# Splitting each of the last two output stores into one of 119 rows and one of 9

## The chip, the cores and the metric

The kernel runs on one core of one Trainium2 chip. The metric is device time in microseconds (us) of one execution, as the median of several runs. One further execution was recorded by the hardware profiler; its page and its trace are what the readings below come from.

## What is computed

Two blocks follow each other. The first is a gated linear attention over 4 batches, 8 heads, 768 steps and head size 48. The second projects its output to 2 x 512 channels, runs a decaying sum over time on one half, gates it with the other half and projects back to 384 columns.

```
# attention: q, k, v, alpha are (B=4, H=8, S=768, D=48)
for t in range(S):
    state = alpha[:, :, t, :, None] * state + einsum('bhd,bhe->bhde', k[:, :, t], v[:, :, t])
    y[:, :, t] = einsum('bhd,bhde->bhe', q[:, :, t], state)
x = y.transpose(0, 2, 1, 3).reshape(B, S, H * D)          # (4, 768, 384)

# gated state-space block: w_in (384, 1024), A_log (512,), w_out (512, 384), float64 weights
val, gate = split(x @ w_in)                                # two halves of 512
h = exp(A_log) * h + val[:, t, :]                          # for every t; ys[:, t] = h
out = (gate * sigmoid(gate) * ys) @ w_out                  # (4, 768, 384) float32
```

Only the last lines matter for this change: the output is 4 x 768 rows of 384 float32 values, 1536 bytes a row, contiguous in DRAM.

## The kernel before

The work is cut into N = 12 groups of GC = 256 time steps (three groups for each batch), and each group into two chunks of C = 128 rows. The function `fast` writes out by hand one order of instructions for all engines; nothing reorders them afterwards. Each engine takes its own instructions in that order and waits on semaphores where data come from another engine or from a DMA. The attention of group m = n + 1 is interleaved with the state-space block of group n, so that TensorE always has matmuls to do. For the last group, n = 11, there is no attention left, and only the state-space block runs.

For each group, `output(n)` is called last. It takes two accumulators `os[0]` and `os[1]`, one for each chunk of 128 rows, and multiplies the gated hidden state `fs[n]` by `w_out`: the first three of four blocks of 128 channels in `part(range(split))`, the fourth in `finish()`. `finish` then copies each accumulator into an SBUF tile `o_sb` of 128 partitions x 384 values and stores it by a DMA that the SyncE queue (SP) issues:

- For all groups but the last, ScalarE does the copy (line 839) and SP stores it (line 842).
- For the last group, VectorE does the copies (line 841), and SP stores them with the same line 842.

The stores are line 842 throughout: 24 of them, two for each group, each of 128 rows. Each row is one packet of 1536 bytes for a DMA engine, and each engine that takes part in a transfer ends its share with a packet of 4 bytes, which counts up the semaphore of that transfer. Transfers that SP issues use a handful of semaphores in turn; in the program those of the last two stores are number 104 and number 107.

After the last group, `fast` returns a flag that was computed on the way: whether the inputs lie in the range for which this fast path is exact. The caller branches on it:

```
    with tc.manual_schedule():
        good = fast(tc, *args)
    with tc.If(good <= 0):
        general(tc, *args)
```

The flag is good here, so every engine jumps over the whole of `general` with one branch instruction (line 1059). At the target of that branch SP waits, one semaphore after the other, until every DMA has landed (line 1059), then for the other engines (line 1086), and then all engines meet at a last barrier. This is how the program ends; nothing is computed after the two copies of line 841.

Of the kernel before, what the change touches and what calls it, by code (L numbers as in the profile page):

```python
# [346 lines left out]
def fast(  # L347
# [18 lines left out]
    nc = tc.nc  # L366
# [3 lines left out]
    C = 128  # L370
    G = 2
    GC = G * C
    NG = S // GC
    N = B * NG
# [20 lines left out]
    def mm(*dims, b=None):  # L395
        return ps.tile([C, *dims], FP32, tag=f"b{b or next(next_mm)}", name="mm")
# [427 lines left out]
    def output(n):  # L824
        b, g = divmod(n, NG)
        os = [mm(DM) for c in range(G)]

        def part(ccs):
            for c in range(G):
                for cc in ccs:  # L830
                    nc.tensor.matmul(os[c], fs[n][:, cc, ds(c * C, C)], w_out[:, cc, :],  # L831
                                     start=(cc == 0), stop=(cc == NI - 1))

        def finish():
            part(range(split, NI))
            for c in range(G):
                o_sb = p3.tile([C, DM], FP32, tag="o_sb", name="o_sb")
                if n < N - 1:
                    nc.scalar.activation(o_sb, os[c], AF.Copy)  # L839
                else:  # L840
                    nc.vector.tensor_copy(out=o_sb, in_=os[c])
                nc.sync.dma_start(out=out[b, ds(g * GC + c * C, C), :], in_=o_sb)

        split = NI - 1 if n else NI // 2
        part(range(split))
        return finish
# [244 lines left out]
```

## Time and profile before

| what | value |
|---|---|
| median of 3 runs | 295.99 us (295.86 to 297.54) |
| the profiled execution, its own time | 295.81 us |
| its span, first to last instruction | 294.1 us |
| TensorE busy | 280.9 us, 96% of the span |
| mean granted TensorE clock | 0.998 |
| stores of line 842 | 24 of 192 KB each |

The span is what the views of the profile are counted in: time 0 is its first instruction. The difference between the profiled execution's own time and its span, 295.81 - 294.1 = 1.7 us, lies around the span. In the views, PE is TensorE, PEld its weight loads, DVE VectorE, ACT ScalarE, POOL GpSimd and SP SyncE; a q after the name means the engine's instruction queue, for instance a DMA that SPq issues. DMA transfers are shown by queue: the q1 transfers are those that SP issues, and the queues called instruction bring the engines their own program. A row "DMA" in digits gives the mean busy share of the core's 16 DMA engines in tenths, in 40 equal slices of the window that is shown.

### The profile page before, as it was taken

To read this page: it belongs to the slowest core of one execution; us is meant where nothing else is said; L and a number is where in the kernel's file an instruction comes from. 1 tells how busy PE (TensorE), PEld (TensorE's weight loads), DVE (VectorE), ACT (ScalarE), POOL (GpSimd) and SP (SyncE) were. 2 spreads that over 40 slices of the span, in tenths; PEclk is the share of its full clock that TensorE was granted. 3 is DMA by queue.
4 is the path that set the end of the run, shared out by engine and by line. 5 is a ranking of instruction groups with operands and counts; after the bars stand their busy time and mean duration, and the time that the engine had idled before them with its cause. 6 is when DMAs were issued, how large, how long until landed. Compare 5 with 4: busy or idle time off the path is not lost.

```text
span 294.1 us, 6126 instructions
## 1 busy us (share of the span) xinstructions
PE 280.9 (96%) x2345; PEld 226.1 (77%) x2345; DVE 224.9 (76%) x269; ACT 99.5 (34%) x220; POOL 113.7 (39%) x116
## 2 busy tenths in 40 slices
PE   7679999999999999999999999999999999999991
PEld 6468877886886896886886896886886886886870
DVE  5898896999996799798699699699699695312311
ACT  2447634433432432432432431431431531331110
POOL 7136792275612612642613513542513523401110
PEclk9999999999999999999999999999999999999999
DMA  9999979999991991991991792991891401101101
GB/s 130 163 175 285 356 128 168 234 271 217 264 177 54 237 167 33 244 187 39 246 171 31 199 213 48 228 196 33 226 204 29 111 10 33 54 15 28 54 7 61
DMA packets 71231, 42.09 MB, mean 143 GB/s; under 512 B 47492, under 2 KB 70536, under 8 KB 71192
## 3 DMA queue, kind: packets, MB, share of 16 engines
q1 hardware_dynamic: 69760, 40.96, 68.5%
q0 software_dynamic: 384, 0.44, 0.7%
q8 instruction: 20, 0.33, 0.5%
q10 hardware_dynamic: 1048, 0.20, 0.4%
q14 instruction: 19, 0.16, 0.2%
HBM read 33.33 MB, written 4.72 MB: 129 GB/s over the span
## 4 chain that ended last, share of the span: by engine, by line
PE 91%; DVE 6%; ACT 1%; issue 0%; DVEq 0%; ACTq 0%
PE mm L801 44%; PE mm L831 21%; PE pair L717 8%; PE pair L745 7%; PE pair L756 3%; PE st L766 3%; PE mm L707 2%; PE st L880 1%; DVE Z L610 1%; PE pair L595 1%; DVE inv L642 1%; DVE prod L664 1%; DVE inv L681 1%; DVE A L734 0%; DVE prod L632 0%
## 5 line engine op out<-in xcount | busy, mean ns | idle before, releaser
L801 PE MATMUL mm<-xT,w_in 128*128 128x256 f32 x576 | 131.1, 384 | 0.0
L801 PEld LDWEIGHTS mm<-xT,w_in 128*128 128x128 f32 x576 | 107.3, 190 | 18.1 <-issue 2.0
L817 POOL TENSOR_TENSOR f<-sg,hh 128x256 f32<-128x256 f32 x48 | 59.0, 1230 | 96.3 <-DVE hh L809 48.6
L831 PE MATMUL mm<-w_out,f 128*128 128x384 f32 x192 | 64.4, 487 | 0.0
L730 POOL TENSOR_TENSOR A<-A,mask 128x512 f32<-128x512 f32 x24 | 30.0, 1271 | 66.6 <-ACT A L729 66.6
L831 PEld LDWEIGHTS mm<-w_out,f 128*128 128x128 f32 x192 | 36.2, 190 | 23.1 <-POOL w_out L555 0.6
L816 ACT ACTIVATE sg<-mm 128x256 f32<-128x256 f32 x48 | 18.4, 384 | 93.9 <-PE mm L801 91.8
L809 DVE TENSOR_TENSOR_SCAN hh<-a_dec,hh,mm 128x256 f32<-128x256 f32 x32 | 23.2, 726 | 20.2 <-PE mm L801 20.1
L734 DVE TENSOR_TENSOR A<-pair,mask 128x512 f32<-128x512 f32 x24 | 16.1, 688 | 27.5 <-ACT A L729 17.7
L664 DVE TENSOR_TENSOR_SCAN prod<-aT,first 128x1024 f32<-128x1024 f32 x10 | 28.1, 2811 | 0.1
L717 PE MATMUL pair<-Z 48*128 48x128 f32 x384 | 25.1, 279 | 1.2 <-DVE first L660 0.9
L685 DVE TENSOR_TENSOR_SCAN inv<-aT,last 128x1025 f32<-128x1025 f32 x10 | 26.0, 2596 | 0.3
L717 PEld LDWEIGHTS pair<-Z 48*128 48x128 f32 x384 | 22.6, 187 | 3.5 <-issue 2.1
L839 ACT ACTIVATE o_sb<-mm 128x384 f32<-128x384 f32 x22 | 10.8, 491 | 42.8 <-PE mm L831 42.8
L745 PE MATMUL pair<-A,v 128*64 128x128 f32 x352 | 21.3, 274 | 0.0
L745 PEld LDWEIGHTS pair<-A,v 128*64 128x64 f32 x352 | 19.1, 137 | 0.0
L650 DVE STREAM_TRANSPOSE aT<-raw_a 128x1024 f32<-128x1024 f32 x9 | 18.4, 2041 | 0.0
L650 DVE STREAM_TRANSPOSE Z<-raw_q 128x1024 f32<-128x1024 f32 x9 | 18.2, 2020 | 0.0
L650 DVE STREAM_TRANSPOSE Z<-raw_k 128x1024 f32<-128x1024 f32 x9 | 18.1, 2015 | 0.0
L729 ACT ACTIVATE A<-pair 128x512 f32<-128x512 f32 x24 | 13.3, 598 | 7.0 <-PE pair L717 5.7
L766 PEld LDWEIGHTS st<-v,ktm 128*64 128x64 f32 x320 | 11.4, 137 | 3.9 <-issue 3.0
L769 ACT ACTIVATE S_sb<-st 128x192 f32<-128x192 f32 x20 | 6.6, 331 | 19.8 <-PE st L766 11.1
(119 smaller groups left out, 255.3 us busy)
## 6 DMA issues: line engine op xcount, KB each, us to landing
raw_k<-in_k_dram SPq DMA_DIRECT2D x24, 192.0 KB, 5.4
raw_q<-in_q_dram SPq DMA_DIRECT2D x24, 192.0 KB, 6.2
v<-in_v_dram SPq DMA_DIRECT2D x24, 192.0 KB, 6.4
out_dram<-o_sb SPq DMA_DIRECT2D x24, 192.0 KB, 1.9
raw_a<-in_alpha_dram SPq DMA_DIRECT2D x23, 192.0 KB, 4.0
raw_a<-in_alpha_dram SPq DMA_DIRECT2D x18, 176.0 KB, 4.2
raw_k<-in_k_dram SPq DMA_DIRECT2D x18, 176.0 KB, 5.7
raw_q<-in_q_dram SPq DMA_DIRECT2D x18, 176.0 KB, 6.6
```

The costliest lines, as they stand in the source:

```text
L650: nc.vector.transpose(out=to.rearrange("p h (c j) -> p h j c", j=NT), in_=raw_bufs[m % NR][name].rearrange("p h (j d) -> p h j d", d=D)[:, ...
L664: nc.vector.tensor_tensor_scan(out=prod, data0=al, data1=first.rearrange("p h n -> p (h n)"), initial=0.0, op0=ALU.mult, op1=ALU.max)
L685: nc.vector.tensor_tensor_scan(out=inv[:, ::-1], data0=aT[:, ::-1], data1=lasts[:, 0:4 * GC + 1][:, ::-1], initial=0.0, op0=ALU.mult, op1= ...
L717: nc.tensor.matmul(sc[i][:, p, :], Z[rows, p, 1, cols], Z[rows, p, 0, cols], start=True, stop=True)
L730: nc.gpsimd.tensor_mul(A[:, 1], A[:, 1], mask_all())
L745: nc.tensor.matmul(ys[m][i][ds(64 * s, 64), e, ds(c * C, C)], v_sb[:, c, 2 * p + i, :], A[:, i, p, :], start=(c == 0 and e == 0), stop=Fal ...
L766: nc.tensor.matmul(st[ds(64 * i, 64), p, :], ktms[c][:, p, i, :], vs[m % NV][:, c, 2 * p + i, 0:D], start=(ch == 0 and p == 0), stop=(ch = ...
L801: nc.tensor.matmul(pj, w_in[cc][:, kk, vg, :], xT[:, kk, :], start=(kk == 0), stop=(kk == NK - 1))
L809: nc.vector.tensor_tensor_scan(out=hh, data0=a_dec[:, cc:cc + 1].to_broadcast([C, GC]), data1=pv, initial=prev_h[cc][:, GC - 1:GC] if n % ...
L816: nc.scalar.activation(sg, pg, AF.Silu)
L817: return lambda: nc.gpsimd.tensor_mul(fs[n][:, cc, :], sg, hhs.pop((n, cc)))
L831: nc.tensor.matmul(os[c], fs[n][:, cc, ds(c * C, C)], w_out[:, cc, :], start=(cc == 0), stop=(cc == NI - 1))
```

## The change

For the last group (n = N - 1 = 11), each store of 128 rows becomes two stores of the same tile: rows 0 to 118, and rows 119 to 127. All other groups keep one store for each tile. Which bytes go where is unchanged, and so are the copies ahead of the stores.

```
                 else:
                     nc.vector.tensor_copy(out=o_sb, in_=os[c])
-                nc.sync.dma_start(out=out[b, ds(g * GC + c * C, C), :], in_=o_sb)
+                rows = [C] if n < N - 1 else [119, 9]
+                for i, size in enumerate(rows):
+                    at = sum(rows[:i])
+                    nc.sync.dma_start(out=out[b, ds(g * GC + c * C + at, size), :], in_=o_sb[ds(at, size)])
```

In the instruction order that results, SP issues four stores in place of two ahead of its branch: 119 rows of the first tile, which waits for the first copy of line 841; 9 rows of the first tile; 119 rows of the second tile, which waits for the second copy; and 9 rows of the second tile. Each of the four has a semaphore of its own, the four next ones in the turn. The instructions of all other engines are the same in number and order, with line numbers 3 higher behind the change.

## Prediction

> **What bounds the kernel now.** I read the page first, for its chain of work that ended last; then the stores' own line; then the DMA view of two short windows, one around the last two stores and one around the two before them; last the waits of SP at the end.
>
> ```profile
> span 294.1 us, 6126 instructions
> PE 280.9 (96%) x2345; PEld 226.1 (77%) x2345; DVE 224.9 (76%) x269; ACT 99.5 (34%) x220; POOL 113.7 (39%) x116
> PE 91%; DVE 6%; ACT 1%; issue 0%; DVEq 0%; ACTq 0%
> ```
>
> TensorE sets the time for nearly the whole span. The chain of work ends with the two copies of line 841, and the timeline of the end shows them and the two stores behind them:
>
> ```profile
> 287.17 1.26 DVE L841 COPY o_sb<-mm 128x384 f32<-128x384 f32 x2 [4.99 <-PE mm L831]
> 287.76 1.03 SPq L842 DMA_DIRECT2D out_dram<-o_sb  x2
> ```
>
> The copies end at 287.17 + 1.26 = 288.43 us, the span at 294.1. So 5.7 us are a tail in which no engine computes. The change lies wholly in this tail: no matmul hides anything there, and nothing before 287.76 can be touched.
>
> What is in the tail? The DMA view of the window from 288 to 294.1 us (each digit is 0.1525 us), and below it that of the pair of stores before, from 271 to 275 us (each digit 0.1 us):
>
> ```profile
> DMA  0001999439894001100000000100100000000000
> q1 hardware_dynamic: 288, 0.39, 19.1%
> q8 instruction: 1, 0.02, 1.7%
> out_dram<-o_sb SPq DMA_DIRECT2D x2, 192.0 KB, 3.8
> ...
> DMA  0000000000000000179999439898920000000000
> q1 hardware_dynamic: 288, 0.39, 27.7%
> out_dram<-o_sb SPq DMA_DIRECT2D x2, 192.0 KB, 1.9
> ```
>
> The reader is to see two blocks of nines, one for each store, some 0.65 us each: all 16 DMA engines work. The undisturbed pair lands 1.9 us after its issue. The last pair takes 3.8 us, though its blocks of nines end as soon (288 + 13 x 0.1525 = 290.0 us): what follows is a trail of zeros and ones, one or two engines of 16. The packet records of the trace show it singly. 30 of the 32 counting packets of 4 bytes start by 289.97; the two others of the second store start at 290.575 and 291.682. The engine that is last sends its eight rows of the second store from 291.192 to 291.621, a row each 61 ns. Its share of the first store ends at 291.187, against 289.27 on fourteen other engines. In that stretch the trace has a program fetch of 16384 bytes from 288.701, 1.631 us long, which overlaps it. That this fetch shares the late engine is my reading; the engines have no number in the records. Of SP's wait at the end the view of waits says
>
> ```profile
> SPq L1059 <- SPq L1059: 3.1, 3, 2.1
> L1059 SPq EVENT_SEMAPHORE  x8: 17/17/17, 289.3 to 292.4; - x8
> ```
>
> SP passes the first store's semaphore at 291.685 and the second's at 292.147, 0.46 us after its last counting packet began. The rest, 294.08 - 292.15 = 1.93 us, is a fixed ladder of 60 to 90 ns checks and the last barrier.
>
> [...] 288 packets for two stores are 256 rows and 2 x 16 counting packets. [...] 16384 and 8192 byte fetches follow the branches of line 1059. [...]
>
> **The change part by part.**
>
> *Issue on SP.* Two DMA instructions more. A store takes 332 ns when the one before it is done; the 48-row, 16-row and 32-row transfers of line 787 that follow each other take 590 and start each 640 ns. So the 9-row store issues from about 288.13 to 288.75 and the second 119-row store, whose copy ends at 288.43, starts at 288.75 in place of 288.46: 0.3 us late. The last 9-row store issues at 289.4, the branch follows at 290.0 in place of 288.84. SP comes back from its branch 0.5 us later (289.345 - 288.84), 290.5, and would have to wait until 291.685 anyway: cost nothing, the cover being the late DMA engine, 1.2 us of it. [...] unknown, from 0 to 0.28 us (the 4-row load of line 861 took 0.864 us, the load issued next to it by SP 0.582); I take 0.1, and it is also covered.
>
> *The data on the first seven engines.* First packet 0.825 us after the issue (288.581 - 287.756). The first store's 17 rows take 17 x 61 ns = 1.04 us, to 289.62; in before 8 rows, 0.49. Its 9-row sister adds one row. The second store's first packet would be due at 288.75 + 0.83 = 289.58, as the first ends; 17 more rows to 290.65, one more to 290.75. An undisturbed engine of the seven thus ends at 290.75 to 290.9, against 289.97 in before: 0.8 to 0.9 us later, but still 0.8 before the late engine.
>
> *The late engine.* This decides, and the trace of before doesn't say where it lies. If it is one of the first seven, it has 2 x (17 + 1) = 36 rows in place of 16: 20 x 61.3 ns = 1.23 us more. The bound below: it was busy for 291.68 - 288.58 = 3.10 us, of which 16 x 0.061 = 0.98 were rows; the other 2.1 are the fetch and gaps. With more rows to fill gaps, and a fetch of 1.0 (the short end of the other 16384-byte fetches: 0.875 to 1.8 us), 36 x 0.061 + 1.0 = 3.2 us, +0.1. I take +0.9, nearer the top, because the rows came after the fetch rather than between. If it is one of the last seven, it has no row at all and the end passes to the others.
>
> *The ladder.* The last two semaphores move from the fourth and fifth of eight checks to the sixth and seventh, since four stores take the next four in turn. What is left to do after the last wait falls by two checks of about 80 ns: -0.16.
>
> Sum for the likeliest: 295.81 + 0.9 - 0.16 = 296.55, say 296.5. The profiled execution stands 0.2 below the median of 295.99; I keep its frame.
>
> **The rivals.**
>
> 1. *The late engine has no share any more, or the second late one is decisive.* With neither of the two late engines in the first seven, the last row lands by 290.85, SP passes at 290.85 + 0.46 = 291.3 in place of 292.15: -0.85 - 0.16 = -1.0, 294.8 us. If only the second one is (290.575 in before), it ends at 290.575 + 1.23 = 291.8, as late as now: 295.8. For it: 9 of 16 engines lie outside the first seven. Against: nothing shown, but the records leave it open. A gain beyond 1.0 us is excluded: SP's fourth issue and the landing after it are needed anyway.
>
> 2. *A store of 119 rows isn't spread at all.* 119 and 9 are odd; if the engine count had to be a power of two, all 256 rows would go through one engine: 256 x 61.3 ns = 15.7 us from 288.58, the last row at 304.3, SP passes at 304.7 in place of 292.15: +12.6 - 0.16, so 308.2 us, slower by 4%. It decides once the late engine has some 64 rows in place of 16: 48 x 61.3 ns = 2.9 us, one per cent. For it: no transfer of before has an odd row count. [...]
>
> 3. *The edit costs its issue time in full.* If SP's four issues ended the kernel, the last at 289.4 plus up to 3 x 0.28 = 290.2 and a landing of 1.9 us, the end is 291.3 to 292.1 in place of 292.15 at SP's wait: 295.6 at most. It would show as SP waiting on the fourth store alone.
>
> **How the numbers follow.** Likeliest, the late engine in the first seven: 0.52, 296.5 us, own range 295.7 to 297.2. Rival 1: 0.32, 294.8 to 295.9. Rival 2: 0.11, 308. Rival 3: 0.05. The range takes in the first, rival 1 and 3 and the spread of single runs of before, whose highest was 1.5 above the median: 294.6 to 297.8; rival 2 is left out. A difference within 1% (2.96 us) is about what a measurement of this kernel can tell from no change. The likeliest and rivals 1 and 3 lie within it; slower by over 1% is rival 2 with a little for a worse backlog, 0.12; faster by over 1% would need 3 us of a 5.7 us tail of which 1.93 are the ladder and 1.9 the landing: 0.02; within 1%: 0.86.
>
> **What would show it.** In the changed profile, 256 rows of 1536 bytes and 2 x (7 + 9) = 32 counting packets show k = 7 and 9 at once; 2 x 2 = 4 counting packets would show single engines. The DMA digits after 288.5 us should stand at 4 (7 of 16) in place of 9, for some 2.2 us. Landing of the stores: about 2.4 us undisturbed, over 4 on the late engine. SP's branch moves to about 290. I am wrong if the digits stand at 0 for more than 5 us, if any line before 287.7 us shifts by more than 0.5 us, or if the span differs from 294.1 by over 2 us with 32 counting packets.

## The result and the profile after

The changed kernel takes 296.87 us (median of 20 runs, 296.6 to 297.99), against 296.12 us for the kernel before in 20 runs beside it. The ratio is 1.0033 with a 95% interval of 1.0022 to 1.0045: slower by a third of a per cent, which is 0.98 us; the two medians lie 0.75 us apart. The forecast was 296.5 us, "within 1%".

The head of the page of the changed kernel, and the timeline of its end:

```profile
span 295.1 us, 6128 instructions
PE 281.5 (95%) x2345; PEld 226.8 (77%) x2345; DVE 224.9 (76%) x269; ACT 99.3 (34%) x220; POOL 113.5 (38%) x116
```

```profile
287.24 1.26 DVE L841 COPY o_sb<-mm 128x384 f32<-128x384 f32 x2 [4.99 <-PE mm L831]
287.82 1.47 SPq L845 DMA_DIRECT2D out_dram<-o_sb  x4
```

Two instructions more, the two DMAs. The copies end at 288.50 in place of 288.43 us: all work before the stores is where it was, and the 1.0 us lies in the tail. SP needs 1.47 us for four issues; two took 1.03. Next, the DMA view of the same window as before, 288 to 294.1 us, 0.1525 us a digit:

```profile
DMA  0300542734334445554344320000000020001000
q1 hardware_dynamic: 288, 0.39, 22.2%
q14 instruction: 4, 0.03, 1.6%
q8 instruction: 1, 0.02, 1.0%
out_dram<-o_sb SPq DMA_DIRECT2D x2, 178.5 KB
out_dram<-o_sb SPq DMA_DIRECT2D x2, 13.5 KB
```

There are 288 packets again: 256 rows and 32 counting packets, 2 x (7 + 9). Once the rows go out, the semaphores of the four stores (104, 107, 108, 109) have 7, 9, 7 and 9 updates, one for each counting packet. So 119 rows go out on seven engines, 17 rows each if they share evenly, and 9 rows on nine. The prediction reckons with these counts; no store before the change showed them, and they were an assumption of mine. The digits stand at 3 to 5 in place of 9, so seven or so of the 16 engines work, and they work until 291.7 us in place of 290.0. And SP's waits:

```profile
SPq L1062 <- SPq L1062: 3.6, 2, 3.1
SPq L1089 <- PEq L1089: 0.7, 2, 0.5
```

Two waits in place of three, the longest 3.1 us. (Line 1062 is the branch, 1059 before.) The instruction records of the trace tell which of SP's checks it stands before, in us from the start of the span:

```
                          before     after
SP, first store issued    287.756    287.823
SP, branch                288.840    289.344
SP checks semaphore 100   289.345    289.865
                    102   289.445    292.987   <- after: stalls here
                    103   289.540    293.083
                    104   291.685    293.172   <- before: stalls here (its first store of line 842)
                    107   292.147    293.257
                    108   292.236    293.328
                    109   292.321    293.402
                    110   292.392    293.468
VectorE back from branch  291.332    292.408
last counting packet      291.682    292.387
```

The stall of 3.1 us in the changed kernel stands before the check of semaphore 102. That semaphore belongs to the group before, whose first store had landed 16 us before (its last counting packet is at 273.4 us). So SP isn't waiting for a store there. What fits is that it has no instruction to execute: a fetch of 8192 bytes of program starts at 291.462 us, and SP goes on 1.52 us after it. In the kernel before, the trace has the last update of semaphore 104 at 291.668, 17 ns before SP passes it. That wait did end with a store; a fetch could be hidden under it.

### The profile page after: what moved, and what is told of

Read it like the earlier page. It is cut to its first block, busy times and chain, and to the rows that moved or that the text cites. A ratio compares the mean times of both kernels' runs of the same rounds, so it can differ in the third digit from the quotient of the medians.

```text
span 295.1 us, 6128 instructions
## 1 busy us (share of the span) xinstructions
PE 281.5 (95%) x2345; PEld 226.8 (77%) x2345; DVE 224.9 (76%) x269; ACT 99.3 (34%) x220; POOL 113.5 (38%) x116
## 5 line engine op out<-in xcount | busy, mean ns | idle before, releaser
L766 PE MATMUL st<-v,ktm 128*64 128x48 f32 x320 | 13.0, 224 | 0.3 <-ACT ktm L708 0.3
```

Source lines behind the costliest of these rows:

```text
L766: nc.tensor.matmul(st[ds(64 * i, 64), p, :], ktms[c][:, p, i, :], vs[m % NV][:, c, 2 * p + i, 0:D], start=(ch == 0 and p == 0), stop=(ch = ...
```

## The experiments

Three theories of the 1 us were set against each other: *landing* (the last row lands later), *issue* (two more DMA instructions on SP), and *fetch* (the program fetch behind a branch is held up by the rows). The edits below change either the row counts of the last two stores, `rows = [C] if n < N - 1 else [119, 9]`, or the branch. Some later expectations put a second question: why a store on few engines is slower than its rows.

### Four stores, all on 16 engines

```
-                rows = [C] if n < N - 1 else [119, 9]
+                rows = [C] if n < N - 1 else [112, 16]
```

> The last two stores are split into 112 and 16 rows: four stores as in the change, but each row count divides by 16. Three theories of the 0.75 us that the change cost. (Fetch) SP's program fetch behind its branch is held up by the longer lists of rows on few DMA engines, 1.3 us in the changed kernel: here all 16 engines have 7 + 1 rows a store as before, so SP's second check at the branch target comes at 291.7 to 292.2 us in place of 292.99, and the time is 296.1 to 296.4. (Landing) The last row lands later on a busy engine: here it lands as before, the last counting packet starts at 291.6 to 291.8, time 296.1. (Issue) Two more DMA instructions on SP delay its branch by 0.5 us and all that follows: here the cost is the same as in the change, 296.9.

Measured: 297.3 us, ratio 1.0062 (1.004 to 1.0084) to the kernel before: by the median more than the change itself, though the two intervals touch, and outside what any of the three said. There are 64 counting packets, 4 x 16, so all 16 engines carry rows of each store. The timeline has the reason for the time:

```profile
287.83 2.90 SPq L845 DMA_DIRECT2D out_dram<-o_sb  x4
```

```profile
L845 SPq DMA_DIRECT2D out_dram<-o_sb x26: 338/368/1414, 56.8 to 290.3; - x26
```

Four issues take 2.90 us, as one of them, the second, takes 1414 ns in place of some 340 (the columns are the shortest, the median and the longest). SP branches at 290.780 and gets past its stall at 293.501, 2.72 us later. The end of the kernel follows SP's branch, not the rows. *Landing* falls as the sole cause: the last counting packet is at 291.742, as early as in the kernel before.

### All rows on one engine

```
-                rows = [C] if n < N - 1 else [119, 9]
+                rows = [C] if n < N - 1 else [127, 1]
```

> The last two stores are split into 127 rows and 1 row[...]. Every theory: 4 counting packets in place of 32, 256 rows at 61 ns = 15.7 us from 288.6, last row at 304.3, SP passes at 304.8, time 308 us. What tells apart: (Fetch) if the program fetches of DVE and SP run on the one engine that carries the rows, both come back from their branches late, by up to 7 us; if they run on others, both come back EARLIER than in the kernel before, DVE at 290.6 in place of 291.33 (2.6 us behind its branch, as ScalarE and GpSimd need without stores) and SP's stall behind its branch is 2.1 us or less; (Landing, Issue) the come-back times stay as in the changed kernel, 292.4 and 293.0.

Measured: 309.07 us, ratio 1.0441 (1.0419 to 1.0462). There are 4 counting packets, one a store, and the rows follow each other by 61 ns: one engine carries them all. From the view of line 1062, with the times of branch and come-back last but one on each row:

```profile
L1062 DVEq COMPARE_BRANCH  x1: 72/72/72, 288.0 to 288.0; - x1
L1062 DVEq EVENT_SEMAPHORE  x1: 21/21/21, 290.9 to 290.9; - x1
L1062 SPq COMPARE_BRANCH  x1: 50/50/50, 297.5 to 297.5; - x1
```

VectorE comes back at 290.941 us, 0.39 us earlier than in the kernel before and 1.47 earlier than in the changed one: with the rows on a single engine, its fetch starts 1.03 us after its branch, against 1.55 and 2.56 us. SP's branch is late only because its second and fourth issue took 2.4 and 6.5 us; it is past its stall 2.78 us after the branch. From its first check to its second it takes 2.26 us, against 3.12 in the changed kernel; 2.1 or less had been expected, and 290.6 for VectorE. So both come back earlier, as *fetch* said, if by less than it said; the one engine isn't one that brings VectorE's or SP's fetch.

### Without the branch

Both kernels without the two lines that branch to the general path:

```
     with tc.manual_schedule():
         good = fast(tc, *args)
-    with tc.If(good <= 0):
-        general(tc, *args)
+    del good
```

> The kernel before without the fallback branch: the general path is left out, and no engine jumps at the end. Fetch: with no jump there is no program fetch to wait for at the end, and no fetch that shares an engine with the stores: the second store lands 1.9 us after its issue at 288.46, the trail of ones in the DMA digits is gone, SP passes at 290.4 in place of 292.15, time 294.3 us or a little less. Landing alone (the late engine being late for a reason of its own): the trail stays and the time is 296. Issue: no view on it.

> The changed kernel without the fallback branch: the general path is left out, as in its partner, so that the two differ by the change alone. Fetch: the cost that comes through the program fetch is gone, and what is left is the landing on seven undisturbed engines: the last row starts by 290.9 in place of 290.0, so 0.8 to 0.9 us over the partner, about 295.1, with SP waiting on the last of the four semaphores. Landing: the same 0.8 to 0.9. Issue: 0.5 to 0.75 over the partner, with SP's last check following its last issue by the same 1.9 us as in the partner.

Measured: 293.12 us without the split and 294.89 with it, 1.77 us apart. The DMA view from 288 to 294.1 us, first of the unsplit kernel, then of the split one:

```profile
DMA  0000599919997000000000000000000000000000
out_dram<-o_sb SPq DMA_DIRECT2D x2, 192.0 KB, 1.9
```

```profile
DMA  0000543634344535454444210000000000000000
q1 hardware_dynamic: 288, 0.39, 21.7%
```

The trail of ones of the kernel before is gone, together with the fetches: the stores land in the 1.9 us of an undisturbed pair. So the late engine of the prediction was late through a fetch. The packet records of the kernel before agree: eight rows in a run, its share of the first store, start from 290.316 us on, as a fetch of 16384 bytes ends (290.332). I take that fetch for TensorE's: it starts 0.66 us after TensorE's come-back from the branch (288.040), and without the branch it is absent. The branch costs the unsplit kernel 2.8 us (295.9 us for the kernel before in the runs beside it). Not all of this is fetching: from SP's pass of the last store's semaphore to the end of the span it takes 1.11 us here and 1.94 with the branch, so 0.8 us lie in the checks behind the landing. The forecast of 294.3 had not counted these. But for the split kernel, both forecasts of its landing, 0.8 to 0.9 us over its partner, were half of what came. Its last counting packet is at 291.724, where I had worked out 290.9. Without the branch nothing hides this, and the change costs 1.77 us; with it, 0.75, by the medians in either case.

### Count of stores against count of engines

The kernel without the branch, with stores of 112 and 16 rows.

> Without the fallback branch (the general path is left out) and with stores of 112 and 16 rows: four stores, all on 16 engines. Its partners are the unsplit and the 119 and 9 kernels without the branch, 293.12 and 294.89 us. (Few engines) The 1.8 us between them come from rows crowding on seven engines: here the rows are spread, the last lands 0.4 us later than unsplit since SP issues four stores, time 293.3 to 293.6, and the second issue, which took 1.41 us with the branch, takes 0.3 to 0.6, as there is no program fetch on the engines. (Count of stores) Two more transfers cost the time by themselves: 294.6 to 295, and the second issue takes 1.4 us again.

Measured: 293.9 us, 0.8 above the unsplit one, where 0.2 to 0.5 was expected. The second issue takes 419 ns; the stall of 1.4 us went with the branch. SP's last issue starts 1.33 us after its first in place of 0.70, which is 0.63 of the 0.8. For 119 and 9 rows the same distance is 1.12, so issuing accounts for 0.42 us of its 1.77; and from the last issue to the last passed semaphore it needs 3.26 us in place of 1.90: the other 1.36 us come with the few engines.

### Why few engines are slower than their rows

Two pairs of stores on nearly the same number of engines: both kernels have 16 counting packets, which fits 2 x (5 + 3) and 2 x (4 + 4). *Ports* stands for a guess of mine, that engines hold each other up or not by which rows of the tile they read at the same time: with 124 rows they would, with 125 they wouldn't. No run shows a ground for it.

```
+                rows = [C] if n < N - 1 else [125, 3]      # one kernel
+                rows = [C] if n < N - 1 else [124, 4]      # the other
```

> Without the fallback branch (the general path is left out), stores of 125 and 3 rows: five engines with 25 rows each, then three with one. In the 119 and 9 kernel without the branch, rows of the first microsecond took 125 to 150 ns in place of 65. (Ports) [...] the rows take 65 ns from the start, some 16 rows in 200 ns, and the first store's rows are sent in 1.55 us. (Slow start) A store on few engines starts slowly whatever its partitions: rows of 120 ns or more for the first microsecond here too, under 11 rows in 200 ns, first store's rows sent in 2.2 us or more.

> Without the fallback branch (the general path is left out), stores of 124 and 4 rows: four engines with 31 rows each. (Ports) [...] rows of 100 to 130 ns throughout the first store, 7 to 9 rows in 200 ns, first store's rows sent in 3.3 to 3.7 us. (Slow start) After the first microsecond the rows take 65 ns, 13 rows in 200 ns, first store's rows sent in 2.5 us.

Measured: 295.66 and 296.93 us. The DMA views from 288.5 to 292.5 us, 0.1 us a digit, of 125 and 3 rows, then of 124 and 4:

```profile
DMA  0322342413232325222423324323233233242110
GB/s 0 108 61 77 92 77 92 108 31 92 61 92 77 123 92 108 77 108 108 154 92 123 138 92 154 123 108 138 108 138 138 108 138 138 92 154 92 46 61 15
```

```profile
DMA  0340306200331233212221222223132222322322
GB/s 15 77 77 15 46 31 46 15 0 15 108 61 61 77 61 77 61 46 108 77 61 61 108 92 108 92 92 123 61 123 77 92 108 77 123 92 92 123 92 77
```

Both start slowly. With 125 rows, 9 to 12 rows go out in 200 ns for the first microsecond, each about 100 ns long, then some 16, each 65 ns; *ports* said 16 from the start. With 124 rows it is 1 to 10, then up to 14. *Ports* falls as the explanation of the start by its forecast for 125 rows. The 124 rows, on one engine fewer, do start worse, but the records don't tell which rows an engine sends, so why they do isn't shown. *Slow start* had the shape right and was too mild on the worst of it (rows of over 300 ns).

Two more kernels without the branch, one which splits only the second of the two stores, and one which leaves out the 9-row stores:

```
+                rows = [119, 9] if n == N - 1 and c == 1 else [C]   # second store alone
+                rows = [C] if n < N - 1 else [119]                  # no 9-row stores
```

> Without the fallback branch (the general path is left out), only the second of the last two stores is split into 119 and 9 rows; the first is whole. In the changed kernel without the branch the first 119-row store ran at half rate (10 to 13 rows in 200 ns on seven engines, rows of 125 to 150 ns) and the second at full rate (22 to 25, 65 ns). (Start of a store on few engines) The seven engines begin together here for the second store: its rows start at half rate too, and its last counting packet is near 1.7 to 2.0 us after its first row. (First of four) What is slow is the first store behind a pause, or while SP issues three more: the second store, with one issue behind it, has rows of 65 to 70 ns from the start, and 18 rows are sent in 1.1 us. Time 293.5 to 294.2 in either case, over 293.12 unsplit.

> Without the fallback branch (the general path is left out), the last two stores have 119 rows each and the last 9 rows of each tile are not stored. (Few engines) The half rate of the first store is its own: rows of 125 to 150 ns for the first microsecond here as well, 0.1 us less than with the 9-row stores, 294.7. (Small stores in between) The 9-row stores[...] slow the rows down: without them the rows take 65 ns, the last lands 0.9 us earlier, 294.0.

Measured: 295.07 and 294.69 us. The first is 0.9 us above the upper end of what was expected. In these two profiles the copies lie 0.7 and 1.3 us later than in the unsplit kernel without the branch, so the windows are 289 to 293 us; second store alone first:

```profile
DMA  0007899971546324744244444320000000000000
GB/s 0 0 0 246 323 384 353 369 261 46 108 77 92 61 61 108 123 77 77 77 154 154 169 184 154 138 77 31 31 0 0 0 0 0 0 0 0 0 0 0
```

```profile
DMA  0000000014453263523454453553543534421000
GB/s 0 0 0 0 0 0 0 0 31 108 77 77 92 46 138 61 92 61 123 154 184 169 154 200 138 169 184 138 154 138 138 200 138 169 169 77 62 15 0 0
```

In the first, the whole store runs at 246 to 384 GB/s, then the 119 rows at 46 to 123 GB/s for a microsecond and at 154 to 184 after it. So it isn't the first store of four that is slow, but the start of a 119-row store whose seven engines begin together, whichever of the two it is. In the second kernel the slow microsecond is there without any 9-row store. The second 119-row store has none of its own: from 290.9 to 292.5 us the view stands at 138 to 200 GB/s. Its engines may be out of step by then, for in the changed kernel the first store's seven shares are counted at seven times, from 290.325 to 291.975 us. From SP's first issue to the last store's semaphore it takes 2.60 us unsplit, 3.85 with the second store split, 4.04 without the 9-row stores, 4.38 with both split. As a guess, rows of engines in step that get into each other's way would fit, but not alone: the engines of a 128-row store begin together too (in the kernel before, 39 rows start in the first 0.2 us), and without the branch their rows take 68 to 71 ns from the start. Nor is it the small number of engines alone. In the kernel of 112 and 16 rows without the branch, all 16 engines carry the first store, and its rows take 91 to 95 ns in the first 0.4 us. The cause stays open.

### One late branch in place of two

The unsplit kernel; ScalarE copies and stores the last group itself, so that SP and VectorE branch before the stores start.

```
-                if n < N - 1:
-                    nc.scalar.activation(o_sb, os[c], AF.Copy)
-                else:
-                    nc.vector.tensor_copy(out=o_sb, in_=os[c])
-                nc.sync.dma_start(out=out[b, ds(g * GC + c * C, C), :], in_=o_sb)
+                nc.scalar.activation(o_sb, os[c], AF.Copy)
+                engine = nc.sync if n < N - 1 else nc.scalar
+                engine.dma_start(out=out[b, ds(g * GC + c * C, C), :], in_=o_sb)
```

> The kernel before, unsplit, but for the last group ScalarE makes both copies and issues both stores itself, so that VectorE and SP, with nothing left to do, take their branch before the stores start. Fetch: the end of the kernel before is two come-backs from a branch (VectorE 291.33, SP 291.69) and a landing held up by fetches (292.15). With one late branch in place of two, ScalarE comes back 2.6 us after its last issue at some 288.9, 291.5, SP's checks wait only for landings at 290.4 to 291, and the end is the barrier behind ScalarE at 291.6: 293.5 to 295 us, 1 to 2 below before. Landing: the late engine stays late, SP passes at 292.1, time as before, 296. Issue: the same as before.

Measured: 295.86 us, ratio 0.9998 (0.9983 to 1.0013): no gain. The DMA view, 288 to 294.1 us:

```profile
DMA  0005799700399940000000000000010010000000
q8 instruction: 1, 0.02, 1.3%
out_dram<-o_sb ACTq DMA_DIRECT2D x2, 192.0 KB, 3.2
```

ScalarE comes back 2.78 us after its branch, at 291.914, and the stores still land late, the last counting packet at 291.230. The one fetch that is under way before 290 us is that of 16384 bytes from 288.557, behind TensorE's branch, so one DMA engine is still held up by it, as it seems. SP passes the last store's semaphore at 291.694, 0.45 us earlier than in the kernel before, but then stalls for 0.39 us ahead of its last check, a semaphore that had long been full. The gain I expected forgot TensorE's fetch and set the come-back too early.

### How long a fetch waits

Two more kernels with the branch, with 9 and with 31 rows an engine:

```
+                rows = [C] if n < N - 1 else [117, 11]     # 13 engines, 9 rows each
+                rows = [C] if n < N - 1 else [124, 4]      # 4 engines, 31 rows each
```

> Stores of 117 and 11 rows, with the branch: 13 engines with 9 rows each, then 11 with one. In the changed kernel the fetch behind SP's branch started 2.12 us after the branch, in the kernel before 1.06; the difference is 17 rows of 61 ns, one engine's share of a store. (Fetch behind a share) A fetch waits for the share its engine has begun: at most 9 x 61 = 0.55 us here. SP's branch at 289.35 as in the change, its fetch at 290.4 to 290.95, its come-back at 292.0 to 292.55 in place of 292.99; the late engine has 20 rows in place of 16 and is done at 291.9; time 296.2 to 296.6, so below the change. (Issue) Four issues on SP cost what they cost, however the rows are spread: 296.9 as in the change. If the second issue stalls for 1.4 us, as it did for 112 and 16 rows, the time is 297.3 for either.

> Stores of 124 and 4 rows, with the branch: four engines with 31 rows each. (Fetch behind a share) If the engine that brings a fetch is one of the first four, the fetch waits for up to 31 x 61 = 1.9 us (or more where rows are slower), so it starts 2.5 to 3.5 us behind its branch; if it is not, it starts 1.0 to 1.1 us behind it, as with 127 rows on one engine, and the come-back is 2.7 us behind the branch. A fetch that starts 2.1 us behind the branch again, as in the change, would speak against the share of rows as the cause. Landing: the last row at about 293.7 as in the same stores without the branch, SP passes at 294.2 or later, time 297.5 to 299.

Measured: 296.97 us, ratio 1.0033 (1.0016 to 1.0049), and 298.95 us. The first has 48 counting packets, which fits 2 x (13 + 11); the stores of the second have 16 without the branch, which fits 2 x (4 + 4). The runs of the first spread from 295.76 to 298.51, and its profile (297.77 us) has again an issue that stalls, the third, for 1.98 us, seen in the timeline and in the late branch:

```profile
287.82 3.23 SPq L845 DMA_DIRECT2D out_dram<-o_sb  x4
```

So its time doesn't decide between the theories; its VectorE fetch can still be read. Of the second, the view of line 1062:

```profile
L1062 DVEq COMPARE_BRANCH  x1: 72/72/72, 288.0 to 288.0; - x1
L1062 SPq COMPARE_BRANCH  x1: 50/50/50, 289.3 to 289.3; - x1
L1062 DVEq EVENT_SEMAPHORE  x1: 21/21/21, 292.8 to 292.8; - x1
```

With the fetch packets of all kernels, from the packet records (a fetch is given to an engine by the come-back that follows it, 1.84 to 1.95 us after it on VectorE, 1.52 to 1.79 on SP; with 117 and 11 rows SP's can't be told from VectorE's next one):

```
                        rows of a   branch    fetch     wait    over 1.05
                        share                 starts
before   VectorE         8          287.893   289.443   1.55     0.50
112/16   VectorE         7          287.964   289.696   1.73     0.68
117/11   VectorE         9          287.957   289.822   1.87     0.82
after    VectorE        17          287.961   290.516   2.56     1.51
124/4    VectorE        31          287.970   290.891   2.92     1.87
127/1    VectorE       127          287.961   288.994   1.03     -
before   SP              8          288.840   289.896   1.06     -
112/16   SP              7          290.780   291.848   1.07     -
after    SP             17          289.344   291.462   2.12     1.07
124/4    SP             31          289.324   290.423   1.10     -
127/1    SP            127          297.516   298.597   1.08     -
```

An unhindered fetch starts 1.03 to 1.10 us after the branch. Where it is hindered, the excess is near one engine's share of rows for 8 rows (8 x 61 = 0.49 us) and, on SP, for 17 (1.04). VectorE's excess for 7, 9 and 17 rows is above these products; they fall into the slow start of the first store. More direct are the counting packets, with which an engine ends its share: VectorE's fetches with 7, 8 and 9 rows and SP's with 17 each start 3 to 6 ns after one. These fetches waited until a share was done.

With 31 rows it is otherwise, although 31 x 61 = 1.90 lies near the measured 1.87. VectorE's fetch starts at 290.891, before the first of the four engines ends its share (291.222). Bytes moved from 290.7 to 291.3 us, 0.015 us a number (102 is one row, 205 two):

```profile
GB/s 0 102 205 0 102 102 205 0 102 102 205 0 546 102 205 0 0 102 205 0 0 102 205 0 0 102 205 0 0 102 205 0 0 205 0 205 0 0 205 205
```

Four rows go out in every 61 ns, one from each engine, and from the fetch on (546) three, until it is done at 291.200. So the fetch runs on one of the four engines, in the middle of its share. Of the 154 rows that start after 291.19, 132 belong to the stores that follow the first and 8 to the shares that end at 291.347 and 291.576; 14 of its 31 are left for the engine of the fetch, which ends its share last, at 292.435. The fetch waited for no more than 17 rows of that engine; rows of the slow start, of up to 351 ns, can have made the wait as long as it was. That 1.87 us agree with 31 rows is chance, and why the fetch went ahead where it did isn't shown.

With 31 rows on four engines VectorE's fetch waits and SP's doesn't; with 127 rows on one, neither does. If a fetch of the same engine runs on the same DMA engine in all these kernels, which no record shows, VectorE's runs on one of the four of 124 rows and not on that of 127; SP's on none of these, but on one of the seven of 119 rows, which the change burdens with 17 rows in place of 8 (1.07 us of wait in the changed kernel, none in the kernel before). The starts of the fetches were as the theory forecast. Its measure, one whole share, held for 7 to 17 rows and not for 31.

## Why the prediction was right, point by point

- *That all is in the tail, and within 1%*: right. The copies end 0.07 us later; TensorE's 281 us are as they were.
- *k = 7 and k = 9*, the numbers of engines that carry 119 and 9 rows: an assumption that no store before the change showed, and right, 32 counting packets. Which seven they are isn't shown; the sums behind its "first seven" need only that the same seven carry all four stores. Rival 2, all on one engine, isn't what the change does; tried for itself it took 309.07 us, against its 308.2.
- *The late engine among the first seven, +0.9 us*: right as to the landing. In the changed kernel a long run of rows 61 ns apart ends in two counting packets at 292.320 and 292.387, one row apart: an engine with a share in both the last stores, hence among those it calls the first seven. It ends 0.70 us later than in the kernel before. Rival 1 needed it elsewhere. Whether it is the same engine as before, the records don't tell. The prediction's "30 of the 32 counting packets" by 289.97 are 29; the one left out is the late engine's first, at 291.187, which its text names further on, and no sum changes by it.
- *The undisturbed engines, done by 290.75 to 290.9*: wrong. The term "17 rows take 17 x 61 ns" was mis-sized: in the first microsecond, the seven engines, which start together, need 120 to 150 ns a row without the branch; in the changed kernel the rows of that microsecond take 131 ns on average (65 to 431), against 70 in the kernel before. All the others were done at 291.66; without the branch the last is done at 291.724. It had no effect on the end, since the late engine was later still.
- *Issue on SP, 590 ns each, branch at 290.0, +0.1 an issue for an unknown*: too dear. The three further issues take 287, 274 and 342 ns, and the branch is at 289.344, 0.50 later than before in place of 1.16.
- *"Cost nothing, the cover being the late DMA engine"*: wrong, and it is the step that failed. I took SP's first check at the branch target (289.345) for its return. The stall after the third check did end with the first store, as read; but a fetch of the next piece of program ran under it. Where nothing is in the way of SP's fetch, SP is past its stall 2.72 to 2.80 us after its branch; from the branch at 288.840 that is 291.56 to 291.64, just before the store's 291.685. The changed profile shows the stall bare, before a semaphore that had long been full. In the kernel before, the second store's semaphore at 292.147 set the end, so there was 0.4 us of cover and not 1.2 (without that wait SP would have passed it one check after 291.685, at 291.77). In the changed kernel the branch is 0.50 later and the fetch starts another 1.06 later: SP is back at 292.987.
- *The ladder, -0.16*: right. From the check of the last store's semaphore to the end of the span it is 1.94 us in the kernel before (294.08 - 292.147) and 1.75 in the changed one (295.15 - 293.402).

The sum shows how the errors met. In the changed kernel the last of the four semaphores has its last update at 292.950, so the landing would have let SP pass it at 292.97. SP passed it at 293.402, as it was still doing the checks behind its stall: 0.44 us later than the landing asked for. Forecast for that pass: 292.147 + 0.9 = 293.05. The landing came 0.1 us earlier than forecast and the pass 0.44 later than the landing, so the pass lay 0.35 us above the forecast. With the ladder of 1.75 us, the landing alone would have made the span 0.64 us longer (292.97 + 1.75 in place of 294.08), and the fetch adds 0.43. The number is right, but partly by luck, as the end was set by a term that had been put at nothing.

Two things stay open. Why seven engines that begin together need twice the time for a row: 125 rows on five engines start slowly too (about 100 ns a row), and it isn't the number of engines alone, as 112 rows on 16 show (91 to 95 ns). And why one of four issues stalls for 1.4 us with 112 and 16 rows, and for 2.0 with 117 and 11, and not with 119 and 9: the first stall is absent without the branch (419 ns), so a program fetch in flight has a part in it, but what blocks the issue wasn't isolated.

## What to carry to other kernels

A store at the very end of a kernel costs its landing time, here 1.9 us undisturbed and 3.8 in the kernel before, where one DMA engine finished 1.7 us after most of the others. Splitting it cost 1.77 us on seven and nine engines and 0.8 on all 16, where no branch hid it, so it is better not split at all. This program ends in a branch, and SP, which issues the last stores, branches last (0.95 us after VectorE in the kernel before, 1.38 in the changed one): in such a kernel, count the 2.8 us measured here from its branch beside the landing, and add the rows that its fetch may have to wait for (here up to 17 on its DMA engine). And before a stall in front of a row of semaphore checks is read as a wait for data, look whether that semaphore was already full.

## What the runs showed of the hardware

- The branch over `general` costs an engine 2.6 to 3.0 us where no rows are in the way of the fetch (ScalarE 2.58 in the kernel before, SP 2.72 with 112 and 16 rows and up to 2.80, VectorE 2.98 with 127 and 1): the fetch starts 1.03 to 1.10 us after the branch on VectorE and SP (0.93 on ScalarE), and the engine runs 1.65 to 1.95 us after that.
- A program fetch waited behind rows of a store on its DMA engine: 0.50 us for a share of 8 rows (VectorE, the kernel before), 1.07 for one of 17 (SP, the changed kernel). With 31 rows an engine VectorE's waited 1.87 us, but went ahead with 14 rows of the share still to come.
- A fetch also held up rows: in the kernel before, one engine sent its eight rows of a store only as a fetch of 16384 bytes ended, 1.7 us after the others had begun.
- SP was held in an issue: 6.5 us for a one-row store behind two stores of 127 rows on the same engine.
- Leaving out the branch saved 2.8 us of 296 in the unsplit kernel: its stores then landed 1.9 us after their issue, undisturbed, and the end behind the landing took 0.8 us less.
- Without the branch, the rows of a 128-row store on 16 engines took 68 to 71 ns from the start; those of 119 rows on seven took 120 to 150 ns for the first microsecond and mostly 65 after it.
